# Broadcasting softmax reciprocals in four transfers, with another written-out instruction order

## The chip, the cores and the metric

The kernel runs on one core of a Trainium2 chip. A core has engines that work beside each other, each on an instruction queue of its own and in the order of that queue: TensorE (PE in the profile) multiplies matrices, VectorE (DVE) and ScalarE (ACT) work element by element and read TensorE's results from its accumulator memory, GpSimd (POOL) works element by element on the main on-chip memory, and SyncE (SP) does nothing here but issue DMA transfers. The transfers themselves run on 16 DMA engines that all queues share. Semaphores tie the queues together. The metric is the device time of one execution in microseconds (us); smaller is better.

## What is computed

A parallel block: attention and a gated feed-forward network read the same normalised input, and both results are added to the residual.

```python
x  = A_x                                  # 1 x 2048 x 512, bf16
xn = _layernorm(x)
# attention, 32 heads of 16
q, k, v = split_heads(xn @ A_wqkv)
p = softmax(q @ k^T * 16**-0.5)           # 32 x 2048 x 2048
attention = merge_heads(p @ v) @ A_wo
# gated network, 512 -> 1792 -> 512
gate = xn @ B_W_gate
h = relu(gate) * (xn @ B_W_up)
out = x + attention + h @ B_W_down
```

## The kernel before

**Tiles and stages.** The 2048 rows are normalised in 16 tiles of 128 and transposed once (`xnT`). Attention goes over four blocks of 512 queries, in each over four groups of eight heads, in each over the even and the odd heads (`ee`): 32 attention blocks of four heads, numbered 0 to 31, each over 16 tiles of 128 keys. For one key tile TensorE makes the scores of the four heads (`score()`). Mostly two heads' scores form a unit of 128 x 1024, whose exponential is one ScalarE instruction (L1418): 706 such units in all. For 159 key tiles (`QUAD_AT`) all four heads' exponentials are made elsewhere: VectorE turns the scores into the bits of an exponential by scale and shift (L1373, four to a key tile), and POOL (L1388) or VectorE (L1392) makes two shifted copies whose sum corrects it. TensorE then multiplies the exponentials by `v_aug`, the values with a column of ones beside them, so that the sum of the exponentials, the softmax's denominator, comes out beside the result. Between these, TensorE does the projections, the gated network and the output rows; all its chains of 128 rows are split into two halves of 64 rows, each half four matmuls of 64 x 32 weights against 512 columns. Such a group of four is called a half product below.

**Normalising a block** (`normalise()`). For each of the first 31 blocks, n = 0 to 30:

1. VectorE copies the accumulated block to `o_sb` (L1251).
2. SP issues a transfer of the four denominator rows into a 128 x 16 tile, `rsum<-o_sb` (L1267).
3. VectorE takes the reciprocals, `rrec<-rsum` (L1268).
4. SP issues a transfer of these to memory off the core, `rec_scr<-rrec` (L1269), 4 rows of 512.
5. SP issues the broadcast `rb<-rec_scr` (L1272): each of the four rows to 32 partitions, 256 KB.
6. POOL multiplies `o_sb` by `rb` (L1280 for even, L1285 for odd blocks; the latter's result is moved by four small transfers, L1289, tile `x_sb<-oT`).

The last block is normalised at the end of the kernel without transfers (`normalise_last()`).

**The order is data.** No engine's queue follows the loops. `PLAN` is a packed string of 8302 places: it says in which order the kernel's 8290 operations and 12 blank matmuls stand, and which buffer each tile gets. `Graph.run()` unpacks it, puts every operation at the end of its engine's queue, and adds the waits that the order and the buffers need. `Graph.emit()` gives semaphores and writes the instructions; a weight load is left out where the half of TensorE holds the weights already. SP has one queue for all 429 transfers, in the plan's order: it waits for what a transfer needs before it issues that transfer or any behind it. Each transfer adds 16 to the semaphore of its stream when it has landed; the broadcasts have the streams `n3`, 0 to 3 by turns.

Scores of units have two places of 128 x 1024 in the accumulator memory, by turns: TensorE writes a unit's scores when ScalarE is done with the unit two before. Everything else shares four places of 128 x 512.

Of the kernel before, what the change touches and what calls it, by code (L numbers as in the profile page):

```python
# [16 lines left out]
S = 2048  # L17
D = 512
H = 32
# [117 lines left out]
    "XK^8Qm=;@6?&E1w4;ASpBH0*GVS2hdWk}{&R_pdr@~(ke#k7!%u$(0<+!aou6u_E)Q2GT?sfe6>R|8P4Qua%7;Q@IQ!S+BB-KEGgL{QdbBek+HIcapk(Gf2zR`j-pmt@A0WXS}IT6tp&%C?9#{Yu5*7@`S4Sw}AG"
    "C{+R~^@-A!(>7YEE%J6pw{zu`E~;X;s}v!nw^3+ZMx)|++8=}5BuO&6a!MyaZ+$b@oo=vpOLm;7Lp(E{hMlx-tVfpEPL0g_i>T{Gxtrubp=e3YGmhew?guE4Wb&7kHcl%i7Ry+%f@nCo)vL_<6~`}1Wv<xfS0+Nn"
    "R4hWQcvR4!ycJWR3(~)YuPeU))(Un816m|0tr?B7vTtJ>J&x|W7?>D@<gExRHnfeFD;%ek6*gPafl}UYRnmm*RS+YuN>xwpe>jCHlqvESg^|C~iO7vk#UYo{#K`Rvs}}6oL@o-Iw$K&(n2Km9<v^EzEZOA7k8OXb"
    "Ko&>ZAdovqKFW|-4HZ$v@r~>?i6w{ZD#i)4TxePI49X@|DN_t=qV6z=O+}2(7|rUKu#y9{plc9iW7%e2VFxYzQ#lnl=$dC;H>OC|ouyRXA1UBe7O!+DD9PtXQl$eIsnTYG(*Z;d5h*id>q1^B{b}XakhNJAV4!pd"  # L140
    "l*4KE(XEzlW2&v-X6i`NaLFemtaUH4mIt#Pld@AlY&Rg21&cX7jA5iN>Gl~)i^!~F1&W>(Rz9bdD%v(t$3m5kTP3KRmeM~H{=ZYzirJ#1Lp`U|<BDELR8U(n9w}#M3Z67bK6wyjVAHuG$BrT@4n1VfMU>>|CWZ|m"
    "0H$pc$IkO4Wv5Msh)CY?ut2c=k8%d496RXpSY~Z3SxHy99hA?8*r|+sB%+XpgtSUt$)`q=ZU{NmlDCpbJ{=&tDrJW#Do0TA0<3%I<P%UCU7{pcX^9<VlH68yKy))8W0=lkfoD5^-Ju903s3|~GF|8pp<@<S!sT;P"
    "mSXa;j&kUxoR`YXrQBh=I*^pZQn^TrO4WF8CowNqR28|lKt-*Q<O<Izw5N3Yv<{0%p>IjoJdj>Ss&qb}><ke*p8-y%vYcJYSuV{~7G4o5LZBQ;Bjq$!ls5!KjFy()zdWT*xocEBqntS^-6CrxWR@fiFrwwDVl$}g"
    "`X!~ekrTHP+x@d+<aB0NupwTn*zAAmsZ^<CNbjmi6`SyX_OTV@AfKNpCku?2{t8lsc9PuLF?1;nr2I@k=>c`8`tq4M%S`q>MADsvb4tfu>2Z%1DnD4N<Q-1>XDdaukt&rDsiId=Dx1=@=`8%`WP<zuNK6MydAOuw"
    "KshubR6L?#bwoa&sMy9=JSL%sX`Jqaf>nOZL9FLh_U4j&+${$Yl-(vhr)537R$c@t>$6f%gosK>XMLbliTmWtQy$kSyF#F>TIr-nk`%v7lHBW5I>MKUh^yd$N(lSkC{^UMZkXa(rH@n&(JDPbtT+bI9hXZL4bMN2"
    "t~e``-KlhjI#{r>${v7-^dXE?u^HE$tH`RzX~}k;IwI5+Sw`QCAdsjKGu=ySm7_>4JC2~|V_Nojfu1Hva_7SiSVVUE^p9<FajQ7{t3YJMSzx8pCZ*e`+{$n|5dBk^MXpj|mvz=vad{{^%9R(S=g91#WTj0s?J_{u"
    "R<I3{SgC;1E+2F%Do_6uHN}4p%2=5YD<1ID6BtEr`B?#{+Z9!ASSqi`Rc<9Kw|q+5s*ppaE>0%c%Kf$6v1xdw0tZSD0u@{fmHPRASwSin<h@P>9moe$712<JSAH&8(Q-=4b6=_QA)_Sg&!C}&$~ht_%^SJEwTG+p"
    "%=4dA)45USuz&Vzm7u2d?o#Ckkvdf?r?eyiS2?{ot^yYvCssUCmkWX<=@6?>k0t#3=d~Kte@lP|B%#K@i##u0a}flCKfGvA4z-^Ndb}+ZK&{uHM~2%7T0JfPtG@3jJVjvl72i{7@Gpd4$pBOBS7e3ILq|c4?t&%$"
# [1326 lines left out]
```

## Time and profile before

| | |
|---|---|
| time, median of 3 executions | 680.99 us (680.63 to 682.62) |
| the profiled execution: its time | 681.0 us |
| its span, first to last instruction | 678.1 us |
| granted TensorE clock | 1.0 of full speed |
| SP's transfers | 429, of them 31 broadcasts of 256 KB |

The profile is of one execution. Its page gives each engine's busy time, the chain of work that ended last, and the costliest groups of instructions; other views of the same trace list who waited for whom, the instructions of an engine in order of time (the timeline), the transfers, and the busy times in chosen stretches. TensorE's matmuls are pipelined and their ends are modelled, so that a busy TensorE need not be at its peak.

### The profile page before, as it was taken

Reading aid. Unit: us, or ns where it says so; the run is one execution under the profiler, and the core shown is the slowest. Engines: PE = TensorE matmul, PEld = TensorE weight load, DVE = VectorE, ACT = ScalarE, POOL = GpSimd, SP = SyncE. Lnnn points to the kernel's source line nnn. Section 1 sums busy time; section 2 is a strip of 40 time slices with the busy share of each in tenths; the row PEclk is TensorE's granted clock in tenths of the full one; section 3 lists DMA queues with packets and bytes.
Section 4 is the critical chain, followed back from the end, with each engine's and each line's share of the span. In section 5 each row is a group of like instructions: output and inputs, shape, how many; then the busy total and the mean of one; then the engine's idle time right before and its main releaser. Section 6 shows DMA issues by size and latency. Waiting matters only on the chain.

```text
span 678.1 us, 46986 instructions
## 1 busy us (share of the span) xinstructions
PE 668.2 (99%) x22358; PEld 392.7 (58%) x21562; DVE 615.1 (91%) x1042; ACT 657.9 (97%) x718; POOL 511.7 (75%) x519
## 2 busy tenths in 40 slices
PE   8999999999999999989999999999999999999998
PEld 3555555566656666555555656555665565565554
DVE  9957899999999999889999989999999899999795
ACT  6999999999999999989999999999999999999995
POOL 3313657877788787888788878888888968888982
PEclk9999999999999999999999999999999999999999
DMA  7321221123121111111111112011112212101121
GB/s 218 66 50 29 60 68 44 47 66 93 47 85 35 48 28 54 39 47 47 51 49 34 52 30 59 17 40 40 58 28 73 61 33 72 39 23 38 33 64 58
DMA packets 55947, 35.97 MB, mean 53 GB/s; under 512 B 19336, under 2 KB 51784, under 8 KB 55752
## 3 DMA queue, kind: packets, MB, share of 16 engines
q1 hardware_dynamic: 55464, 32.71, 17.3%
q8 instruction: 171, 2.80, 1.7%
q10 hardware_dynamic: 288, 0.26, 0.1%
q14 instruction: 24, 0.20, 0.1%
HBM read 26.35 MB, written 2.35 MB: 42 GB/s over the span
## 4 chain that ended last, share of the span: by engine, by line
PE 91%; DVE 5%; DMA 2%; POOL 1%; issue 0%; SPq 0%; ACT 0%; DVEq 0%; POOLq 0%
PE ps L263 91%; DVE qd L1373 1%; DVE stats L758 1%; DVE xn_sb L771 1%; DMA rsum<-o_sb 1%; DMA xnT<-xn_sb 1%; POOL qd L1388 0%; DVE v_aug L909 0%; DMA rec_scr<-rrec 0%; DMA x_sb<-in_A_x_dram 0%; DVE qd L1392 0%; DVE qT L985 0%; DVE kT L902 0%; DVE mv L759 0%; DVE xnT L812 0%
## 5 line engine op out<-in xcount | busy, mean ns | idle before, releaser
L1418 ACT ACTIVATE ring<-ps 128x1024 bf16<-128x1024 f32 x706 | 651.4, 1079 | 6.2 <-PE ps L263 5.3
L1388 POOL TENSOR_TENSOR qd<-qd,ints 128x512 int32<-128x512 int32 x458 | 462.0, 1039 | 131.3 <-DVE qd L1392 81.0
L263 PE MATMUL ps<-qT,kT 64*32 64x512 bf16 x8192 | 466.6, 374 | 3.5 <-DVE qd L1373 2.4
L1373 DVE TENSOR_SCALAR qd<-ps 128x512 int16<-128x512 f32 x636 | 412.3, 684 | 36.2 <-PE ps L263 32.3
L263 PE MATMUL ps<-qd,v_aug 64*32 64x512 bf16 x3816 | 310.3, 375 | 0.1
L263 PE MATMUL ps<-ring,v_aug 64*32 64x512 bf16 x2824 | 244.2, 375 | 0.0
L1353 PEld LDWEIGHTS <-kT 64*32 64x32 bf16 x8032 | 170.9, 92 | 101.7 <-issue 15.5
L1325 PEld LDWEIGHTS <-v_aug 64*32 64x32 bf16 x6004 | 144.8, 92 | 71.8 <-issue 11.2
L263 PE MATMUL ps<-xnT,wgs 64*32 64x512 bf16 x1792 | 140.5, 374 | 0.2 <-DVE qd L1373 0.2
L263 PE MATMUL ps<-xnT,wus 64*32 64x512 bf16 x1792 | 137.3, 375 | 0.4 <-issue 0.2
L1392 DVE TENSOR_SCALAR qd<-qd 128x2048 int16<-128x2048 int16 x89 | 61.9, 701 | 1.2 <-PE ps L263 0.8
L842 PEld LDWEIGHTS <-wus 64*32 64x32 bf16 x1792 | 44.1, 91 | 23.7 <-issue 4.9
L842 PEld LDWEIGHTS <-wgs 64*32 64x32 bf16 x1792 | 43.2, 91 | 22.9 <-issue 3.8
L263 PE MATMUL ps<-Wd,hT 64*32 64x512 bf16 x608 | 55.3, 375 | 0.1
L842 PEld LDWEIGHTS <-hT 64*32 64x32 bf16 x1440 | 35.2, 92 | 21.1 <-issue 4.2
L263 PE MATMUL ps<-Wo_p,x_sb 64*32 64x512 bf16 x480 | 44.8, 375 | 0.0
L1057 DVE COPY up_sb<-ps 128x512 f32<-128x512 f32 x56 | 38.4, 686 | 3.4 <-PE ps L263 3.0
L263 PE MATMUL ps<-Wv,hT 64*32 64x512 bf16 x448 | 41.3, 375 | 0.0
L263 PE MATMUL ps<-Wv,xnT 64*32 64x512 bf16 x576 | 36.7, 374 | 0.5 <-DVE v_aug L909 0.3
L263 PE MATMUL ps<-xnT,Wq 64*32 64x512 bf16 x480 | 37.1, 375 | 0.0
L263 PE MATMUL ps<-xnT,Wk 64*32 64x512 bf16 x480 | 35.8, 374 | 0.3 <-DVE xnT L812 0.3
L263 PE MATMUL ps<-Wk,hT 64*32 64x512 bf16 x384 | 35.8, 375 | 0.0
(73 smaller groups left out, 306.5 us busy)
## 6 DMA issues: line engine op xcount, KB each, us to landing
rb<-rec_scr SPq DMA_DIRECT2D x31, 256.0 KB
wus<-in_B_W_up_dram SPq DMA_DIRECT2D x38, 128.0 KB, 2.9
wgs<-in_B_W_gate_dram SPq DMA_DIRECT2D x38, 128.0 KB, 2.7
xr_sb<-in_A_x_dram SPq DMA_DIRECT2D x16, 128.0 KB, 3.1
qT<-qf SPq DMA_DIRECT2D x120, 16.0 KB, 2.8
out_dram<-xn_sb SPq DMA_DIRECT2D x14, 128.0 KB, 3.2
x_sb<-in_A_x_dram SPq DMA_DIRECT2D x8, 128.0 KB, 2.8
x_sb<-oT SPq DMA_DIRECT2D x60, 16.0 KB, 3.0
```

The costliest lines, as they stand in the source:

```text
L263: return e.add_instruction(mybir.InstMatmult(name=e.bass.get_next_instruction_name(), engine=mybir.EngineType.PE, ins=[e.lower_ap(x), e.lo ...
L758: G.op("DVE", 580, lambda e, m=m: e.bn_stats(stats[:, m, :], xs(m)), reads=[t_xm[m]], writes=[t_st], prio=pr, order=last_xn if m == 4 else ())
L771: G.op("DVE", 320, lambda e, m=m, t=t_n: e.tensor_scalar(xn_sb[:, t.slot, :], xs(m), mv[:, m, 0:1], rstd[:, m:m + 1], op0=ALU.subtract, op ...
L842: e.ldweights(w()[rows, 32 * j:32 * j + 32], tile_position=(rows.start, 32 * j))
L1057: G.op("DVE", 603, lambda e: e.tensor_copy(up_sb[:, tup.slot, :], bank_of(tu)), reads=[tu], writes=[tup], prio=-590)
L1325: e.ldweights(vs(j), tile_position=(64 * half, 32 * j))
L1353: e.ldweights(ks(m), tile_position=(64 * half, 32 * m))
L1373: G.op("DVE", 601, lambda e, j=j, tx=tx: e.tensor_scalar(qd[:, tq.slot, 512 * j:512 * j + 512], ps[:, BANK[tx.slot], :], IBIAS[3], 0.0, op ...
L1388: G.op("POOL", POOL_NS / POOL_PIECES + 60, lambda e, x=x, n=n, c=slice(i * m, i * m + m): e.tensor_tensor(x().bitcast(I32)[:, c], raw().bi ...
L1392: G.op("DVE", 600, lambda e, n=n, x=x: e.tensor_scalar(x(), raw(), float(SHIFTS[n + 1]), None, op0=ALU.add), reads=[ti, tq], writes=[t], p ...
L1418: exp_ops[u] = G.op("ACT", 904, lambda e, tr=tr, k0=k0: e.activation(ring[:, tr.slot, :, :], ps[:, 4 * k0:4 * k0 + 2, :], ACTF.Exp, scale= ...
```

## The change

**The broadcast.** `PIECES = {"n3": 4}`. Where one transfer took a source of [4, 32 copies, 512] to 128 partitions, four transfers take one row each, [32 copies, 512], to 32 partitions. The four are issued one after the other at the broadcast's place in SP's queue; each adds 16 to the stream's semaphore, and who waits for a broadcast waits for 64 where it was 16. The bytes are the same. SP issues 522 transfers where it issued 429.

**The order.** `PLAN` is another one with the same 8290 operations and 12 blank matmuls; `PLAN_OPS` stays. ScalarE's queue is the same in every place. Of TensorE's 5597 places 4745 hold another operation at the same number, of VectorE's 1042 383, of POOL's 515 418, of SP's 429 382; nothing differs ahead of TensorE's place 71, VectorE's 63, POOL's 16 and SP's 22. Most buffers change as well. In the two orders stand:

| read from the two orders | before | after |
|---|---|---|
| half products from one unit's last scores to the next unit's, 705 intervals: mean | 7.81 | 7.81 |
| their standard deviation | 1.32 | 1.11 |
| intervals of 10 or more | 64 | 26 |
| `rsum` transfers at most 2 places behind a broadcast in SP's queue (of 31) | 10 | 2 |
| `rsum` transfers at most 4 places behind one | 16 | 5 |
| blocks with at most 2 units between the plan's places of `rsum` and of its reciprocal | 10 | 13 |
| units between these two for block 11 | 2 | 17 |
| groups of four weight loads on the two halves | 5357 | 5273 |
| TensorE operations behind the last scores | 62 | 61 |

```diff
 CARRIED = []
+PIECES = {"n3": 4}
...
                 if e == "SP":
-                    o.sem = (dsem[o.stream], 16 * (o.val + 1))
+                    o.sem = (dsem[o.stream], 16 * PIECES.get(o.stream[0], 1) * (o.val + 1))
...
-        fin = [(dsem[s], 16 * n) for s, n in streams.items()]
+        fin = [(dsem[s], 16 * PIECES.get(s[0], 1) * n) for s, n in streams.items()]
...
                 ins = o.fn(eng)
                 if e == "SP":
-                    ins.then_inc(o.sem[0], 16)
+                    for piece in ins if isinstance(ins, list) else [ins]:
+                        piece.then_inc(o.sem[0], 16)
...
-            dma(lambda e: e.dma_start(rb[:, trb.slot, :], rec_scr[n].unsqueeze(1).to_broadcast([4, 32, 512])), 520,
+            dma(lambda e: [e.dma_start(rb[32 * j:32 * j + 32, trb.slot, :], rec_scr[n, j:j + 1, :].to_broadcast([32, 512])) for j in range(PIECES["n3"])], 520,
                 reads=[tsc], writes=[trb], prio=pr - 50, stream=("n3", n % 4), name="n3")
```

The lines of the packed `PLAN` string, all but a few of which differ, are left out.

More of the change, by code (lines that the diff above doesn't have):

```diff
@@ L224 @@
[L224 to L226 removed]
+    "c-mcC2|!F;8@}(kGt)Fpi&QGv_dSuNLPGXPSraW}7fEHwPJ}Fd5`~n|A|X-8k}b-<@0GG;-;$Yo|8vg0cgp{vnmcECm*;)n=bY(dn1BD{$v<BDiF}b>kv|Pz;vX9_FNGh(3B2$g`71o;|5=b{s-HD@h5s?H#BHkQ"
@@ new lines @@
+    "OH=53;%?Qu>I@LRG<d}`4T|X;PJG0HWQS-mr!$=w=YnLYZcUyCX(wq9U^rm}(6xpCIELo{|DoeJG6d*;934V_=ER-oL{9eu-jtZela25{o)?3`>4K`WLo}8{{|1E2!n-qcJD#jZCz1yowHr8TM_w|Pz9a+bmOOCM"
+    "hWHsLx=UVBk3>Itx+KpD+Y*m}r+(qE(HF!DAcpYNEi#(UqF!+%jvOP!NX&;A5*kYV-@>NUO<sJH;b<K3roam?$euzRr5N*!?x_%S;KYCn`Jsl9VDn<e=`)TlPUlKF=4h}$T!H!lf|;C<Bq7Ok4dS5|1WUzbsE>jX"
+    "!XOeb2@!$^)Bz0=tQ1F(eMJkzh?1}L4Z$~tcq+avB3aD7XuA|D3F90iMutwrfT7RCN)<NNGGgSA7KwPLai$Z+y~qr$7*Ga8_l3|QI#gU=OfnuTI`~gQbmb-$U(KT9#6rWE77ZlmCMIzbWI(J_4u_itMVvukN47yi"
@@ new lines @@
+    "Qs@uWb%-doiFabgwLF8!7%j;I2O#<^*iV)t?*EmOy`^9XB!L7wc>E6j!_(p;Ka$`G!IKz8M44c;7Id6}?Z%ta$7D5%WFdTXDH>$0SSut~!p=0_40$4^jf6;-907O&P<bIvya+n{PlK@M0x(4EFf`?KJD%DuvH{rz"
+    "n<^xm(=A4$i?^hX;D5wzPK=tsDx#IVt_R>?&{fEHvIp4-KV=XH61iw8m(cmVNP_~vNYMYt$eUV$+=KvYbsQpA6U~PRB914~$HV9o9<M_q#fu(_-1$dAfP<YOE@%;n7k(4xk(Lf8)HOAqM`8d;HiYa776@xmx2PrL"
+    "J4aKA<4iXc!A)lgcoo+bs88Tc3_OBB0hvNX@fR(529<hZPKkx$It06wN*WKbNC=!+Y!Y6Hghw1nCXva%<%mW{h=O1$b&Yt&i<#yncxjP{UYbO$Fo!3sz)?EJjsq?@p^C9p40(x24bti)6-#&H88Ll$9+JvNs0x9L"
@@ new lines @@
+    "gguCxypDTum*NpMTq~rU_#t#cI-F*S8i0g1h2T)|Ndft-BpGMWFMa$~EAS^nK_J#7$rH^ojX3s<#D)?B{(*#$PywEU1T2w)6yhZ;LnEbSgzf_Z#%OVB#g;%FXMm}0>a_K7AQgv1hYXD?FD(fIjSIblCnX^)E=H3P"
+    "V=I`=)F4c$*rXOuyLL4?K-a>g+U7->Au<#7MXXsZlDep19|+Ln1U!o==5-20$TqDsPRk0$k>bO9YFM%u5{pQJmr&MXbC+Ntv@Ov-jf}7M3#wa0wa4@eh(kbV*E)qzQ*w%~))b{eAc<Ru6QvqY)rUa7^c_(<(KL|("
+    "7;%W^NB|D)HR3p$KxuQSElbYulE{=~F<&i189`z(I_&C%A8<M!=|fQt3QeD?AA$!loKQoN3c^leP|*~+v_zA%WPw(Yu7y%%3u57NLgN)XjMUY6QM?H8W(5AG4Fu8VE16515>PoKl$zvxb$hP?S8-jgW+L&E?`mF$"
@@ new lines @@
+    ")S8Ef>ZD7cu7(AbXVqF<)QytJmL!lU79_#TOY&UsUkEiNZz7gOQAt}X4?-K}Xk0+brdE^_f~b-Npcd6Y9Dc@eY<1d2z0T>7$cbSQ<0Yk9hjcO&R}nAjI#KS`=(3X17b6C`<}2`}B=Y%x6@K-LnpmrGN)ltFB_zm6"
+    "Jf}qxr<3SvkSIzC9F)HVj@BYU1Mz~O5W<EeTX~^~s0t986G)7}NF7>aIWfmnI{>9_+8G4G7c{%Tp|n-dg+wVzTQG=vOBzK7kUG|a4w#hJkto6m&(od);?}}JKx}f745O(M)+4wTx&Va??N^M*5d=U;;0R9a7__E9"
+    "1Siq}Cu#$+mjC~(%8PzV=MNGqjZD;ew4rJR+NLJcQzC7gqG}Ub1br+DDY4t}l28<m07BJJ&$YtYf)NN@5Z;7}Ks*Xi@CmC^lHkO-T9y-at)#cb(*Y+Qb3j*<x^o{RN>Wi*iLZsfG*ZAz=LDfy>JB>+1xhCZ(q%Z2"
@@ new lines @@
+    "1qH??$YXg)|B93+0GLBMIZTfiVk9_8xkyc!C(Cl87}pUC$JAs*DMpfW;`s-3R|Xv7#pWT-5|SwuDs7sA4CJNbkaTLH0fA~s0K9IZt`|x`rEVjku0>5*9bDagfe0iC0J^yXgNR2$8g0se0wh4df>x(FL?bCDNKh7f"
+    "BG&S{y46`J6r)5jH5pL%im4_>UT~Dx)h+D^yrfn+>B>bs;(~a7<a7sgv9*xKE(I0DKF&zl;Xoo=t*B51^{u7nR?%fr$6D#2EWE>rYOz|wiani^5T<iYlz^PB>j^<e5<0|wsLO!}y6T}~-zO0fj1>D5uhR@7JMg;x"
+    "B{pNJP3Tk}&okA`U%j=|e;MH*Cj><x9I3tVyr5ZylcA7ff&0Y$1%eSM2pCF;NIKJtlX;<$3L~nupX4|>HHzFU?he8+SEy8u|AzoU=Z&cN2~>5;Uy?)2|KIjWv1Fv`<OEnqmexRLO{H0_keQnDt){H37HoX=iC4Nj"
@@ new lines @@
+    "<g2xgR4Brsfu>KZOQj$Ig&x64_YLAj3s+s1x`UM{*?H+?K#!rkSazZ$)rwL?XbqCl0?qMAx)fuC#>a^VX)(z>=t3>r9EvY>s-T7zuhuAh^&KKtLyQVvr~+U(sFuKjqvDkn=p;~0VyM9!x&TX;VZ3f>Ar^@H_pX;H"
+    "Ql8aH@=omXoY-*jds2e~-8|B+>9K`Dy2=q$3&U!pI}D^tDLFYaf_Bg#sw(gyi4}=KD}qc^bmR<5*QUKf%L}O!4h~c=NO7*#(84CvX5rLI`zmelA~7)1sY85EATOk=GhVvxlp2e4#a(?PEL_AA-9rmWFo9l1iubXM"
+    "a47mK<Ev{2q*H`M%e-*iDdtnU2$s$wBBcljBh#u_;52fcVRZY|=t+pzagfwJB+XLYm<8j=(>InvKf)|h;|L^`zwRnnSG&TEC||>TX)$S8sfP<XO}x}$n7=aNDn^7dFp~1u0<Sxu2pUhg|J0ppsQwVSpxjDo$eiv{"
@@ new lines @@
+    "PRN_C(8Y@!QT&RhY5_OAt`%uTb`X1>bU&lJ36@Gm$7D4%2hZ31WJY%o`=@0v|5xC;4qT&cSAWE#+m2(z_)1XVbS;|J1BhPg_)QR(3@?dB9quSCg47u~;Tl~$U-7~fi-f7_lbsGp;*}%lV!-@!<gRfo05ueMwcj;j"
+    "@(<}(hfYU`|12j}CI>YR`_-Rs@gQASSGNXTDe=J9Xfm8oj)J(TQI5P&MZ!lF;-@;8B7{H)cdU}apxmStMRhg#3ZKD9w~zwc>3D_#(S9uh)qRwax~+8H7jHayRMQWs?@%QwTvACf)aq_<K)k}JsX=PImXx<}AgUpD"
+    "#XiT^Y_~N5SmWd>d`M88xl)^&pD;2t5)L(B!T)<07ut_lcf5GO(~1hGMzhm#hL$K!dOxo_i4de}rQ?No+To?6BZH(QG2#JCssY`3m@Y&Q%2dmWH-3UP5~3<m22S2<8;N*pR4vc{Q`FM^x$a>}J)ZgJnw}SL-gv3y"
@@ new lines @@
+    "la?kOZdhH`pyr*7^cfvJI7&LR#{G<_By<``C$@O0H&);3{ePKO5381ElFVlqMt8SfQ*>23RHKN+4^gY(T76Mi^OGl$L27PT<Ar$nB^}{~@zt7?Jknh()F^*JONkejyzXk27teGxo#Mq${c7%A{aLs$mxq6dTRJA`"
+    ">=QLp&ClJ%Yn6XAF{e9~F?@~k_(!-hLSA|1|8;WB;OMX*g-?1z5<dc*sy|y5kEFcxDX(-bCyF{9J90G{LiepU{QF;t0u+CL0t<*oZGh!imMgH8$@KrQoPHHFdM49j>%c2$SOR)vxP?rsr^SC2_Z!QeBCz~~pUE}&"
+    "3&P*Y03+=uWQNeg#xe!E3$^k4wcsm2eFVne5g6cYSpH_GYh9rL?+FU9L_HG$8uq-{6P>`T;P3bkR08xtv0Z9?H2-RlkJ@pHTWtZlJ^^i0<Iiet<;V%iP`|e3m*Q6`SgW42`TTBST%DgKu-mh}>Wlgl$jq8=Y}9<&"
@@ new lines @@
+    "`Y*q=va17?r}}Wm-wlIWu7Rjay>cVjUr_xvMAMbs42MG1pDg!Nr`8y<aM&disk>VN{P=$PgWE}qimOMV2(m2g^S=$r_Oap7!{3<-6Ex#l3)na;>+irnwN`|vjxK<iliL?+)W6!Q3lA8r04QkkME_5BI8mo=Ny5;2"
+    "RmzIqa2-_@I)!IiLj0aVnX+S9HUr^FBSpKF=;8!L3+OPdUc$2(TNHy}6KrVM-~RFK2WSl3=yaq?qZkDZB2;(LRZm|?OhSHW_wfU}&qJ@Nnl;v({9Tc}4s4lu`QDOXbs(IH7*;vAHn(E&)m`!H!aw(SU4}pt^-W!w"
+    "T?lEb#-iZ0i<Tmzan`UzA05=(TOwZq#rqS-A4G2;D6Gy5=QnS5z(j=FHFZFtNx#2XM_uXoxdf%~$V;R2-_zf;MH6^gZ@e}=zp`0aL}PflsDJN}u}QCP!I?R->*H$ee6scOO_;iPV4wL7V0vOhyOrNZX&&f%@9{6_"
@@ new lines @@
+    "l?M+e8hyP9J@W=_gcnh&%Cq)`(0j|w>6(}=U066iq^QNz7yf(mp{VnDRnX>}Nx3ROSu3(@$EqGg+QrO$1XGH+Q%61x7zk%lhu=K<GGH~FTJ$W{Gk%20cNR`Ymp)URoL$JHR=Wl?U*QHCdC)LlmF(9|`?q`iZ0^{W"
+    "nxorcQ9()I#U?#He=e#Wz}>^cga2%s%R2vA4_9Y!iqlt5MmcI`c|+Hp7dFkgUDUZ_jw#3>@Zyr;wwEnGDvY23+Wuend#Nd71}3+$)8vj$UAElj;*u=eJq<sA?fW-i4m}mV8lT<{g)2tDO}jGJQ(wp2gY(Lh2aP|V"
+    "ya`FaU0&ByTkYthugP@F?|IO-(x(1fO(}GVd>b0!*`gF|lU%KW##q9E9WLim!S3Da|9-+X!%?p$9(dTOsMY4Vpss4}@7znC-}9qVdErcd>*p$ujI*1MqM@%*p+nTfrv^<Lm)YEJadwJ=dwQ-nG^*g9G_@*$8)n_#"
@@ L229 @@
+    "tvt-~n7#}}NlGdoh!Q1s8BzI31*@77$Fj6l*<hT|O)*R9D+C!yGAzf5CKO$dCCY*76zsQP41o%*Ttg*oHkij%B5=u)BrGfyO?q--i%^(=i&{ouq(p=}fyy?7p$Uexrl}?--pRqtk}PAaVk8Zuz#%gtObMid@QT<d"
+    "eJW^#vSAntYdlh}riz9ooMS9VGenq)szw>jJ&Tlt0|}}y0uhx!m}?CPQm~X!2sMP*{{e<{%2x")
 class Pool:
```

171 lines of the change are left out of this document (69 added, 102 removed).

## The prediction

> **What bounds the kernel.** I read the page's busy times first, then the same by stretches of 100 us away from the two ends.
>
> ```profile
> span 678.1 us, 46986 instructions
> ...
> PE 668.2 (99%) x22358; PEld 392.7 (58%) x21562; DVE 615.1 (91%) x1042; ACT 657.9 (97%) x718; POOL 511.7 (75%) x519
> ```
>
> ```profile
> core 0: us, PE busy (x) PEld busy (x) DVE busy (x) ACT busy (x) POOL busy (x), PEclk, DMA share, GB/s
> 50.00:100.00 50.00, 49.94 (x1676) 27.30 (x1652) 42.77 (x68) 50.00 (x55) 26.30 (x28) 1.00 0.19 53
> 100.00:200.00 100.00, 99.72 (x3361) 60.06 (x3249) 95.25 (x159) 99.60 (x109) 78.55 (x78) 1.00 0.22 61
> 200.00:300.00 100.00, 97.81 (x3376) 59.22 (x3176) 91.02 (x151) 97.35 (x106) 82.54 (x82) 1.00 0.16 46
> 300.00:400.00 100.00, 99.84 (x3384) 58.19 (x3252) 96.91 (x162) 98.78 (x108) 80.46 (x80) 1.00 0.15 43
> 400.00:500.00 100.00, 99.82 (x3432) 60.12 (x3296) 91.63 (x151) 99.87 (x110) 86.22 (x85) 1.00 0.15 43
> 500.00:600.00 100.00, 99.56 (x3388) 59.57 (x3244) 93.60 (x154) 99.30 (x109) 84.00 (x84) 1.00 0.18 51
> 600.00:650.00 50.00, 49.49 (x1720) 29.31 (x1660) 43.54 (x71) 49.61 (x55) 43.88 (x44) 1.00 0.14 40
> ```
>
> Two engines are full, TensorE and ScalarE, and they hang together: ScalarE may not run ahead of the scores, TensorE may not write scores more than two units ahead. ScalarE's share says how well the order works, because its queue is nothing but units. The best stretch (400 to 500) starts 110 of them, one each 100/110 = 0.909 us. At that pace 600 us would hold 660 units; the seven rows hold 55 + 109 + 106 + 108 + 110 + 109 + 55 = 652. So a better order can win about 8 x 0.909 = 7.3 us between 50 and 650 us, if its pace were the best one throughout. That is the prize; the change leaves ScalarE's work and queue alone, so nothing else shortens that stretch.
>
> The waits say what breaks the pace.
>
> ```profile
> ACT ring L1418 <- PE ps L263: 5.3, 11, 2.0
> ...
> PE ps L263 <- DVE qd L1373: 2.6, 3, 2.0
> DVE rrec L1268 <- DMA rsum<-o_sb: 2.5, 2, 2.1
> ...
> POOL x_sb L1280 <- DMA rb<-rec_scr: 1.1, 1, 1.1
> ```
>
> The columns are the total, the number of times and the longest. Three waits of 2.0 to 2.1 us are one event: VectorE stands before a reciprocal whose denominators have not landed, so TensorE gets no free place, so ScalarE gets no scores. The timelines of VectorE and SP and the chain that ended last show it.
>
> ```profile
> 288.28 0.68 DVE L1373 TENSOR_SCALAR qd<-ps 128x512 int16<-128x512 f32 x1
> 291.10 0.25 DVE L1268 RECIPROCAL rrec<-rsum 128x16 f32<-128x16 f32 x1 [2.14 <-DMA rsum<-o_sb]
> ```
>
> ```profile
> 285.21 0.58 SPq L1272 DMA_DIRECT2D rb<-rec_scr  x1
> 285.84 0.47 SPq L1118 DMA_DIRECT2D out_dram<-xn_sb  x1
> 286.35 0.59 SPq L1267 DMA_DIRECT2D rsum<-o_sb  x1
> ```
>
> ```profile
> 286.35 4.72 DMA rsum<-o_sb
> ```
>
> The `rsum` transfer, 8 KB, took 4.72 us; it was issued 1.14 us behind a broadcast. The other 8 KB transfer of the chain, `rec_scr<-rrec`, took 2.4 us at the median and 3.6 at most:
>
> ```profile
> DMA to landing us min/median/max: 1.4/2.4/3.6
> ```
>
> **The broadcast in four.** A stretch in which a broadcast moves almost alone shows how it runs today.
>
> ```profile
> 78.10:80.90 2.80, 2.80 (x98) 1.76 (x89) 2.02 (x4) 2.80 (x5) 1.90 (x2) 1.00 0.25 94
> ```
>
> In 2.80 us 94 GB/s moved, 263 KB: the 256 KB of the broadcast and little else. The DMA share is 0.25, so a quarter of the 16 engines worked, four of them, full the whole time. A small transfer that needs one of these four stands behind up to 2.8 us of packets; that is the 4.72 less the usual 2 or so. [...] By my own terms I only need that a broadcast cannot hold four engines longer than it does now.
>
> When does the whole broadcast land? The pieces follow each other by the pitch of issue, 285.84 - 285.21 = 0.63 us, so the last goes out 3 x 0.63 = 1.9 us after the first. Its own landing is bounded by the nearest transfers:
>
> ```profile
> rb<-rec_scr SPq DMA_DIRECT2D x31, 256.0 KB
> wus<-in_B_W_up_dram SPq DMA_DIRECT2D x38, 128.0 KB, 2.9
> ...
> qT<-qf SPq DMA_DIRECT2D x120, 16.0 KB, 2.8
> ```
>
> Between 2.8 and 2.9 us, so 1.9 + 2.9 = 4.8 us from the first issue. Today the packets alone end 80.90 - 76.75 = 4.15 us after the issue of this broadcast at 76.75 (its row stands here), and the landing is later still.
>
> ```profile
> 76.75 0.60 SPq L1272 DMA_DIRECT2D rb<-rec_scr  x1
> ```
>
> The multiply gets its reciprocals when it got them before, to within half a microsecond. POOL waited for a broadcast once, 1.1 us (row above); I cost this at nothing, with 1.1 us either way as bounds. [...]
>
> **What SP pays.** 31 x 3 = 93 more issues at 0.63 us are 59 us on SP's queue. They lie beside SP's waits:
>
> ```profile
> SPq L1269 <- DVE rrec L1268: 53.6, 15, 10.6
> SPq L1289 <- POOL oT L1285: 44.9, 10, 8.3
> SPq L892 <- DVE qf L886: 41.2, 10, 12.5
> SPq L1267 <- DVE qd L1373: 38.2, 14, 8.6
> ...
> SPq L1272 <- DMA rec_scr<-rrec: 26.7, 17, 3.2
> ```
>
> The first four alone are 178 us. On average it is hidden. Without cover, each broadcast puts what is queued behind it (query pieces L892, weights L1044, the next `rsum`) 1.9 us later; I take nothing and keep, as the far end, one stall the size of the one seen, 2.1 us. Where SP is early it costs nothing and gains nothing.
>
> **The order.** Term one: the stall at 289 us goes. Block 11's reciprocal has 17 units between it and its `rsum` in the new order, where it had 2; 17 x 0.909 = 15 us cover a transfer of 2 to 5. And 2 `rsum` transfers stand within two places behind a broadcast, where 10 did. I take off the whole 2.1 us. What is late next? At that place nothing in the rows: VectorE's idle time there has no second releaser. The least it can give is 0, if another reciprocal stalls in its stead.
>
> Term two: scores come more evenly. Intervals of ten or more half products between two units' scores fall from 64 to 26, by 59%. In the table 7.3 - 2.1 = 5.2 us are lost beside the stall. If all of it hung on such intervals, 0.59 x 5.2 = 3.1 us come back; if none, 0. I take 1.2, nearer to nothing, because TensorE's own waits are ended by VectorE's evictions and not by a long interval, and VectorE is 91% busy with an unchanged amount of work. Below nothing is possible too: a changed order has its own unlucky places; one event of 2.1 us is the largest seen in 678.
>
> Term three: the ends. The first 71 places of TensorE are the same, and behind the last scores stand 61 operations for 62. I take nothing.
>
> The sum is made against the profiled execution: 681.0 - 2.1 - 1.2 = 677.7 us. Its time equals the median of 680.99, and its span of 678.1 leaves 2.9 us around it that nothing here touches.
>
> **Rivals.**
>
> *A full gain.* Both terms at their best and the pace of 400 to 500 us throughout: 681.0 - 7.3 = 673.7. For it: every measure of evenness in the order improved. Against: VectorE, whose waiting ends score places, keeps its 615 us.
>
> *Hidden, and late elsewhere.* The transfers were hidden anyway (the one wait of 1.1 us), and the stall goes but a weight load comes late, since weights stand behind broadcasts that now take 1.9 us longer to issue. Idle time ahead of weight loads of L842 exists, the longest 2.4 us, though the profile names no releaser for it ("issue"), so that 2.4 is the nearest row and not a proven wait for a transfer:
>
> ```profile
> PEld L842 <- issue: 20.5, 76, 2.4
> ```
>
> One of these gives 677.7 + 2.4 = 680.1, no change that can be measured; also the case in which the new order is simply no better.
>
> *The reciprocal again, slower.* VectorE's queue stalls at every reciprocal whose denominators are late, at up to 2.1 us each. In the new order 13 blocks have at most 2 units (1.8 us) between `rsum` and reciprocal, for 10 before; a broadcast ahead of SP's `rsum` now delays its issue by 1.9 us, which is just that. From 3.3/2.1 = 1.6, so from two such events, the gain is gone; four make 677.7 + 8.4 = 686.1, three 684.0. Against it: ten blocks that tight made two waits in all, of 2.5 us together, and only two `rsum` now follow a broadcast closely.
>
> [...]
>
> **Chances.** The forecast, 675.5 to 678.9, 0.44; the full gain, below 675.5, 0.12; hidden or late elsewhere, 679.0 to 683.0, 0.27; the reciprocal again 0.13; pieces that do not overlap 0.04. About 0.3% (2.0 us) is what a measurement of this kernel can tell from no change. Faster by more: 0.44 + 0.12 = 0.56; within: 0.27; slower by more: 0.17. The range goes from the full gain, 673.7, to 683.0, the upper edge of no change: it leaves out most of the 0.17 and the last of the full gain.
>
> **What would show it.** Right: no wait of VectorE for `rsum` above 0.5 us; 109 or 110 units in the stretch from 200 to 300 us; a DMA share well above 0.25 while a broadcast moves; more than 652 units from 50 to 650 us; 336 fewer weight loads (84 groups of four). Wrong: new idle time before L1268, POOL waiting for `rb` many times, TensorE's weight loads waiting longer for L1044's transfers, or fewer units at equal VectorE time.

## The result, and the profile after

| | before | after |
|---|---|---|
| time, median of 4 executions | 681.81 us (680.63 to 682.88) | 676.35 us (675.45 to 676.5) |
| ratio of the two, 95% interval | | 0.9918 [0.9893, 0.9943] |
| the profiled execution: its time, its span | 681.0, 678.1 us | 675.45, 673.5 us |

The changed kernel is faster by 0.8%, 5.6 us of 681.8. Its lines are numbered two higher than before (L1274 is the broadcast, L1269 `rsum`, L1270 the reciprocal, L1420 the units).

The page of the changed kernel, its busy times, answers to the first lines of the prediction:

```profile
span 673.5 us, 46743 instructions
...
PE 666.5 (99%) x22358; PEld 381.7 (57%) x21226; DVE 616.3 (92%) x1042; ACT 656.0 (97%) x718; POOL 512.5 (76%) x519
```

The work is the same to within 2 us on every engine but one: weight loads (PEld) went from 21562 to 21226, 336 fewer. So the 4.6 us of span are idle time and slow places that are gone, not work. Busy times by stretch, the whole middle in one piece, first the kernel before and then the changed one (the columns are as in the prediction: length, busy time and count of PE, PEld, DVE, ACT and POOL, then the clock, the DMA share and GB/s):

```profile
50.00:650.00 600.00, 596.18 (x20264) 353.76 (x19516) 554.72 (x909) 594.51 (x645) 481.94 (x475) 1.00 0.17 48
```

```profile
50.00:650.00 600.00, 599.87 (x20480) 347.36 (x19412) 560.70 (x917) 598.56 (x652) 486.11 (x478) 1.00 0.18 48
...
200.00:300.00 100.00, 99.94 (x3464) 57.81 (x3184) 93.58 (x154) 99.87 (x109) 85.98 (x85) 1.00 0.17 48
```

ScalarE started 652 units in these 600 us where it started 645, at 0.909 us each 6.4 us. (In one piece a unit that spans an edge of 100 us counts once, so these two numbers are lower than sums over the pieces; by the pieces of the prediction's table it is 661 for 652.) The stretch from 200 to 300 us, 106 before, holds 109. A part of the 6.4 us is given back ahead of it; the stretch from 30 to 50 us, before and after:

```profile
30.00:50.00 20.00, 19.90 (x680) 11.56 (x652) 13.19 (x21) 19.92 (x23) 5.59 (x8) 1.00 0.30 54
```

```profile
30.00:50.00 20.00, 18.35 (x634) 9.93 (x608) 13.31 (x20) 18.61 (x21) 5.29 (x6) 1.00 0.26 62
```

TensorE and ScalarE work 1.3 to 1.6 us less here, and two units fewer start. The waits of the changed kernel name it: VectorE's key copy `kT`, and what ScalarE still waits for in all.

```profile
ACT ring L1420 <- PE ps L264: 2.5, 5, 1.2
...
PE ps L264 <- DVE kT L904: 1.4, 1, 1.4
```

No row for `rsum` or `rb` is left. The issues and landings, after (count, size and median us from issue to landing), with all broadcasts together in the last line:

```profile
rb<-rec_scr SPq DMA_DIRECT2D x124, 64.0 KB, 2.2
...
qT<-qf SPq DMA_DIRECT2D x120, 16.0 KB, 1.9
```

```profile
DMA to landing us min/median/max: 1.9/2.2/3.5
```

A piece lands in 2.2 us though four go out together. The query pieces `qT`, which have nothing to do with the broadcast, land in 1.9 us where they took 2.8. Those issued within 4 us of a broadcast's issue (of its last piece's, in the changed kernel) took 4.1 us at the median before (22 of the 120), the others 2.6; in the changed kernel it is 2.5 (41) and 1.9. Part of that differs from chip to chip: on those of the experiments they took 2.9 us in the new order with one transfer (e2 below) and 2.4 with four (e8).

### The profile page after: what moved, and what is told of

The parts are those of the page before. It is cut to its first block, busy times and chain, and to the rows that moved or that the text cites. A ratio compares the mean times of both kernels' runs of the same rounds, so it can differ in the third digit from the quotient of the medians.

```text
span 673.5 us, 46743 instructions
## 1 busy us (share of the span) xinstructions
PE 666.5 (99%) x22358; PEld 381.7 (57%) x21226; DVE 616.3 (92%) x1042; ACT 656.0 (97%) x718; POOL 512.5 (76%) x519
## 4 chain that ended last, share of the span: by engine, by line
PE 94%; DVE 4%; DMA 1%; POOL 0%; issue 0%; ACT 0%; SPq 0%
PE ps L264 94%; DVE stats L760 1%; DVE xn_sb L773 1%; DMA xnT<-xn_sb 1%; DMA x_sb<-in_A_x_dram 0%; DVE v_aug L911 0%; DVE qT L987 0%; DVE qd L1375 0%; DVE xnT L814 0%; DVE kT L904 0%; DVE mv L761 0%; POOL rstd L755 0%; ACT xn_sb L1219 0%; DVE kT L1001 0%; SPq L689 0%
## 5 line engine op out<-in xcount | busy, mean ns | idle before, releaser
L1420 ACT ACTIVATE ring<-ps 128x1024 bf16<-128x1024 f32 x706 | 649.7, 1129 | 2.9 <-PE ps L264 2.5
L264 PE MATMUL ps<-qT,kT 64*32 64x512 bf16 x8192 | 458.7, 374 | 0.2
L264 PE MATMUL ps<-qd,v_aug 64*32 64x512 bf16 x3816 | 302.0, 375 | 0.0
L264 PE MATMUL ps<-ring,v_aug 64*32 64x512 bf16 x2824 | 242.3, 375 | 1.4 <-DVE kT L904 1.4
L1355 PEld LDWEIGHTS <-kT 64*32 64x32 bf16 x7944 | 163.8, 92 | 105.1 <-issue 14.9
L1327 PEld LDWEIGHTS <-v_aug 64*32 64x32 bf16 x5756 | 138.5, 91 | 73.4 <-issue 11.4
L264 PE MATMUL ps<-xnT,wgs 64*32 64x512 bf16 x1792 | 140.5, 374 | 0.0
L264 PE MATMUL ps<-xnT,wus 64*32 64x512 bf16 x1792 | 137.2, 374 | 0.0
L264 PE MATMUL ps<-Wd,hT 64*32 64x512 bf16 x608 | 54.5, 375 | 0.0
L264 PE MATMUL ps<-Wo_p,x_sb 64*32 64x512 bf16 x480 | 42.8, 375 | 0.0
L264 PE MATMUL ps<-Wv,hT 64*32 64x512 bf16 x448 | 40.9, 375 | 0.0
L264 PE MATMUL ps<-xnT,Wq 64*32 64x512 bf16 x480 | 36.6, 375 | 0.2
L264 PE MATMUL ps<-Wv,xnT 64*32 64x512 bf16 x576 | 36.3, 374 | 0.1
L264 PE MATMUL ps<-Wk,hT 64*32 64x512 bf16 x384 | 35.5, 375 | 0.0
L264 PE MATMUL ps<-xnT,Wk 64*32 64x512 bf16 x480 | 34.0, 374 | 0.4 <-DMA xnT<-xn_sb 0.2
```

The source lines that it names most:

```text
L264: return e.add_instruction(mybir.InstMatmult(name=e.bass.get_next_instruction_name(), engine=mybir.EngineType.PE, ins=[e.lower_ap(x), e.lo ...
L1327: e.ldweights(vs(j), tile_position=(64 * half, 32 * j))
L1355: e.ldweights(ks(m), tile_position=(64 * half, 32 * m))
L1420: exp_ops[u] = G.op("ACT", 904, lambda e, tr=tr, k0=k0: e.activation(ring[:, tr.slot, :, :], ps[:, 4 * k0:4 * k0 + 2, :], ACTF.Exp, scale= ...
```

## The experiments

The twelve kernels ran on other chips than the pair above, where the kernel before took about 687 us; so only ratios to it are compared, and a microsecond below is a ratio times 687. "Old order" is the order before, "new order" the changed kernel's. Moves within an order were made behind the plan, with the buffers that the plan gives: operation x goes right behind operation y.

```diff
+for x, y in MOVES:
+    seq.remove(x)
+    seq.insert(seq.index(y) + 1, x)
```

| kernel | order, pieces | further edit | ratio to before, 95% interval |
|---|---|---|---|
| e1_split_alone | old, 4 | | 0.9965 [0.9933, 0.9998] |
| e2_order_alone | new, 1 | | 0.9936 [0.9914, 0.9958] |
| e3_late_reciprocal | old, 1 | block 11's reciprocal later | 0.9971 [0.9945, 0.9997] |
| e9_split_and_late | old, 4 | the same | 0.9948 [0.9919, 0.9977] |
| e8_after_again | new, 4 | the changed kernel itself | 0.9903 [0.9873, 0.9932] |
| e4_two_pieces | new, 2 | | 1.0110 [1.0079, 1.0141] |
| e11_eight_pieces | new, 8 | | 1.0021 [0.9993, 1.0049] |
| e6_long_intervals | new, 4 | 41 units' scores later | 0.9961 [0.9938, 0.9985] |
| e7_short_intervals | old, 1 | 38 units' scores sooner | 1.0035 [1.0007, 1.0064] |
| e10_split_late_short | old, 4 | e9's edit and e7's | 0.9964 [0.9937, 0.9991] |
| e5_key_copy_first | new, 4 | key copy sooner | 0.9886 [0.9861, 0.9912] |
| e12_three_scores | new, 4 | e5's edit, three scores sooner | 0.9878 [0.9844, 0.9912] |

### The two halves of the change alone

e1_split_alone: the new kernel's code with the plan of before.

```diff
+PIECES = {"n3": 4}
```

> The old order with the broadcast in four pieces. If the order brings the gain and the split only shortens the stall at 289 us (the denominators of block 11 no longer stand behind four full DMA engines, but leave 1.2 us later), VectorE's wait there falls from 2.1 to about 0.5 us and the time by 1 to 2 us: ratio to before 0.997 to 0.9985. If the split itself brings most of it, because all small transfers land sooner, the ratio is near 0.993. If SP's 93 more issues hurt an order that was not made for them, it is above 1.000.

It gained 2.4 us, with an interval from 0.1 to 4.6. By the last step of their semaphores in the traces, no `rsum` transfer took over 2.1 us any more, where 7 of the 31 took over 3 us before. Still the same reciprocal waits, 1.30 us and not the 0.5 that were expected. SP's and VectorE's timelines of e1_split_alone:

```profile
285.22 2.46 SPq L1274 DMA_DIRECT2D rb<-rec_scr  x4
...
288.19 0.60 SPq L1269 DMA_DIRECT2D rsum<-o_sb  x1
```

```profile
290.09 0.25 DVE L1270 RECIPROCAL rrec<-rsum 128x16 f32<-128x16 f32 x1 [1.30 <-DMA rsum<-o_sb]
```

In the old order `rsum` stands behind the broadcast; it now lands in 1.9 us instead of 4.7, and leaves 288.19 - 286.35 = 1.84 us later. Of the stall of 2.14 us, 1.30 are left. The later issue is SP's price, and it shows a second time: `PE ps L264 <- DMA qT<-qf: 1.0, 1, 1.0`, a wait for a query piece that the kernel before does not have.

e2_order_alone: the changed kernel with its broadcast in one transfer.

```diff
-PIECES = {"n3": 4}
+PIECES = {"n3": 1}
...
+            dma(lambda e: [e.dma_start(rb[:, trb.slot, :], rec_scr[n].unsqueeze(1).to_broadcast([4, 32, 512]))], 520,
```

> The new order with the broadcast as one transfer of four rows. If the order brings the gain: ratio 0.993 to 0.995, no reciprocal waiting over 1 us, transfers of 16 KB for the queries landing in 2.8 us at the median as before. If the split is what counts: ratio 0.997 or more, and waits for rsum of 2 us and over are back.

It gained 4.4 us; no reciprocal waits, and the `qT` pieces land in 2.9 us, about as before. The two halves add up: 2.4 + 4.4 = 6.8, and the whole, e8_after_again, gives 6.7; each of the three is known to some 2 us either way.

> The changed kernel once more, unchanged, as the measure for the other three kernels on the same chip: ratio to before 0.989 to 0.994, no reciprocal waiting over 0.5 us, TensorE waiting 1.4 us for the key copy at 35 us.

### The stall by itself

e3_late_reciprocal moves block 11's reciprocal behind the next five instructions of VectorE in the old order.

```diff
+MOVES = ((3450, 3635),)
```

> The old order with one change: the reciprocal of block 11 stands five VectorE instructions later. Term one of the prediction: the 2.1 us stall goes and nothing comes in its place, ratio 0.997 (2.1 us of 681), 108 or more units between 200 and 300 us for 106. Rival: a stall elsewhere takes its place, ratio 0.999 to 1.000.

It gained 2.0 us, with an interval from 0.2 to 3.8. The stretch from 200 to 300 us holds 107 units, one more than before and one less than expected; TensorE works 2.02 us more in it and ScalarE 1.62. Another reciprocal (L1277 in this kernel) has begun to wait, as the rival had it:

```profile
200.00:300.00 100.00, 99.83 (x3404) 59.31 (x3208) 92.52 (x153) 98.97 (x107) 83.67 (x83) 1.00 0.16 45
```

```profile
DVE rrec L1277 <- DMA rsum<-o_sb: 1.6, 1, 1.6
```

e9_split_and_late adds the four pieces, so that the reciprocal is late and all `rsum` transfers are quick.

```diff
+PIECES = {"n3": 4}
+MOVES = ((3450, 3635),)
```

> The old order with the broadcast in four pieces and the reciprocal of block 11 five VectorE instructions later: both repairs of the stall at 289 us and of late transfers, without the new order. If these are most of what the change does: ratio 0.990 to 0.993. If the rest of the new order, its evenness among it, is worth 3 us or more, as the changed kernel with long intervals suggests: 0.994 to 0.997.

No reciprocal waits, and it gained 3.6 us. So what repairs the transfers is worth about 3.6 of the 6.7 us, and 3.1 come from the rest of the order. The two intervals, [0.9919, 0.9977] and [0.9873, 0.9932], overlap a little: the split is rough.

### Two pieces and eight

e4_two_pieces takes two rows to 64 partitions in each of two transfers.

```diff
-PIECES = {"n3": 4}
+PIECES = {"n3": 2}
...
+e.dma_start(rb[64 * j:64 * j + 64, trb.slot, :], rec_scr[n, 2 * j:2 * j + 2, :].unsqueeze(1).to_broadcast([2, 32, 512]))
```

> The changed kernel with the broadcast as two transfers of two rows each. If the outermost dimension (two rows) sets the number of DMA engines, two engines carry everything: about 5.7 us of packets for a broadcast, a DMA share of 0.13 where it moves alone, landings of rsum behind it over 6 us, multiplies waiting for rb, ratio 0.995 to 1.005. If the 64 partitions set it, all 16 engines work: the broadcast lands within 4 us as in four pieces, SP has 62 issues fewer, and the ratio is the changed kernel's.

It is slower than before by 1.1%, and 12 us slower than the same order with one transfer. A stretch, SP's and VectorE's timelines and the waits of e4_two_pieces say why.

```profile
94.00:97.00 3.00, 3.00 (x116) 1.98 (x104) 2.97 (x5) 3.00 (x4) 1.79 (x3) 1.00 0.16 44
```

```profile
95.14 0.60 SPq L1269 DMA_DIRECT2D rsum<-o_sb  x1
```

```profile
101.82 0.25 DVE L1270 RECIPROCAL rrec<-rsum 128x16 f32<-128x16 f32 x1 [2.75 <-DMA rsum<-o_sb]
```

```profile
POOL x_sb L1282 <- DMA rb<-rec_scr: 9.8, 5, 4.1
POOL oT L1287 <- DMA rb<-rec_scr: 4.1, 3, 2.3
DVE rrec L1270 <- DMA rsum<-o_sb: 2.8, 1, 2.8
```

132 KB moved in 3 us, half the rate of before's 263 KB in 2.80 us, with a DMA share of 0.16 where before had 0.25 (0.125 would be two engines of 16; the small transfers are in the 0.16). The ratio is above the whole range that was expected for that case. The `rsum` behind them landed 101.82 - 95.14 = 6.7 us after its issue. The traces show the difference in two more ways. Of the 2 KB packets of a broadcast mostly four move at once in the kernel before (at 78 us), two here (at 94 us), though two transfers are out, and up to 17 in the changed kernel (at 407 us; the records of two packets can overlap a little). And a transfer raises its semaphore in 5 steps before, in 3 here and in 16 as a piece; an `rsum` transfer has 5 steps before and after. So by these runs it isn't the number of transfers that helps: with two, of two packets at once, the kernel is 1.1% slower than before, with four, of 16 steps each, 1.0% faster (e8). The outermost dimension of the source is 4, 2 and 32 in the three; that this dimension sets the number of engines, as the first case of the expectation has it, agrees with the three but was not shown, as no run changes it alone.

e11_eight_pieces takes half the copies of a row in each of eight transfers, 32 KB to 16 partitions.

```diff
-PIECES = {"n3": 4}
+PIECES = {"n3": 8}
...
+e.dma_start(rb[16 * j:16 * j + 16, trb.slot, :], rec_scr[n, j // 2:j // 2 + 1, :].to_broadcast([16, 512]))
```

> The changed kernel with the broadcast in eight pieces of half a row to 16 partitions, 124 issues more on SP. Each broadcast then holds SP for some 4.5 us instead of 2.3. If SP's issues are hidden in its waits: the changed kernel's ratio, 0.990. If what stands behind a broadcast comes late (the price that the prediction put at one stall of 2.1 us for four pieces): 0.993 to 1.000, with waits of VectorE for rsum or of TensorE for query transfers.

It loses 8.1 us against four pieces, more than expected. Each piece still lands in 2.1 us, but SP takes 4.8 us at the median to issue eight, and the whole broadcast lands 7.0 us after its first issue. The waits of e11_eight_pieces are those for the broadcast itself and for things that stand behind it in SP's queue:

```profile
POOL x_sb L1282 <- DMA rb<-rec_scr: 6.1, 4, 2.3
...
DVE rrec L1270 <- DMA rsum<-o_sb: 1.9, 2, 1.6
PE ps L264 <- DMA qT<-qf: 1.6, 1, 1.6
```

So SP's cover of waits, 178 us on its first four rows, bears 93 more issues and not 217, in this order.

### How even the scores come

e6_long_intervals takes the changed kernel and puts the scores of 41 units behind the next two half products, so that 64 intervals of ten or more stand in the order again (standard deviation 1.29, before 1.32).

```diff
+MOVES = ((3555, 2934), (3556, 3555), (2543, 2427), (2544, 2543),
...
```

> The changed kernel with 41 units' scores put behind the two half products that followed them, so that 64 intervals have ten half products or more, as in the old order, for 26. If evenness of the scores is part of the order's gain (term two of the prediction, 1.2 us, or the 2.1 us that such intervals lost less in the changed kernel's trace): 0.002 to 0.005 above the changed kernel's ratio. If evenness is worth nothing, as the old order with shortened intervals suggests: equal to it within 0.001, and the gain of the order lies in its distances to transfers.

Against e8_after_again it loses 0.0058, 4.0 us (some 2.6 either way), with intervals that do not touch, and no reciprocal waits in it. ScalarE's waits for scores, e6_long_intervals and then e8_after_again:

```profile
ACT ring L1429 <- PE ps L265: 6.7, 21, 1.2
```

```profile
ACT ring L1420 <- PE ps L264: 3.9, 8, 1.2
```

(L1429 and L265 are there what L1420 and L264 are here.) 13 more waits, 2.8 us of the 4.0: a score held back by two half products costs 0.1 us on average.

e7_short_intervals does the reverse in the old order: 38 units' scores are pulled ahead, and the intervals of ten or more fall from 64 to 26, as the change has them.

```diff
+MOVES = ((2133, 1724), (2134, 2133), (7660, 7496), (7661, 7660),
...
```

> The old order with units' scores pulled ahead of one to three half products where the interval before them was ten or more: 26 such intervals for 64, as in the new order; the stall at 289 us stays. Term two of the prediction alone: 1.2 us, at most 3.1, ratio 0.9955 to 0.998. Rival: evenness of scores is worth nothing, ratio 0.9993 to 1.001.

It is 2.4 us slower than before, which neither side of the expectation had. Its waits have two reciprocals late, `DVE rrec L1277 <- DMA rsum<-o_sb: 4.5, 2, 2.7`; behind the longer one, 2.70 us, the granted clock was 0.50 for 3.41 us (last section). To take the stall away, e10_split_late_short makes the same moves in e9's kernel, where no reciprocal waits.

```diff
 PIECES = {"n3": 4}
-MOVES = ((3450, 3635),)
+MOVES = ((2133, 1724), (2134, 2133), (7660, 7496), (7661, 7660),
...
+    (3008, 2390), (3009, 3008), (3450, 3635))
```

> The kernel of the run before with units' scores pulled ahead as in the old order with shortened intervals (26 intervals of ten or more half products for 64). If evenness is worth something where no reciprocal stalls: 0.002 to 0.005 below the run before. If it is worth something only in an order made for it, because whatever is put behind the scores comes late in its stead: equal to it or above.

Nothing was gained: 0.9964 beside e9's 0.9948, and one reciprocal waits again, 1.2 us. Holding scores back costs; pulling them ahead, past the work that other engines wait for, brings nothing by itself. The number of long intervals is then not what the rest of the order won by, though it goes with it.

### The head

e5_key_copy_first moves VectorE's key copy ahead of two normalisations in the changed kernel.

```diff
+MOVES = ((166, 158), (179, 166), (177, 179))
```

> The changed kernel with VectorE's copy of the keys (kT) at 35 us ahead of two normalisations of xn instead of behind them. TensorE's wait of 1.4 us there should fall to 0.3 us or less and ScalarE's loss of 1.3 us with it: 1 us, 0.0015 below the changed kernel's ratio. Rival: the normalisations and their transposes come 0.7 us later and give the time back: equal to it.

VectorE's and TensorE's timelines of the changed kernel show what it undoes, and then the stretches, after and e5:

```profile
31.90 3.10 DVE L773 TENSOR_SCALAR xn_sb<-hT,mv,rstd 128x512 bf16<-128x512 bf16 x4
34.92 0.68 DVE L904 CAST kT<-ps 128x512 bf16<-128x512 f32 x1
```

```profile
35.65 0.38 PE L264 MATMUL ps<-ring,v_aug 64*32 64x512 bf16 x4 [1.38 <-DVE kT L904]
```

```profile
30.00:40.00 10.00, 8.48 (x302) 5.04 (x281) 7.54 (x12) 8.78 (x10) 5.29 (x6) 1.00 0.27 56
```

```profile
30.00:40.00 10.00, 9.45 (x328) 5.43 (x316) 7.70 (x14) 9.46 (x11) 5.25 (x6) 1.00 0.40 57
```

In the new order the copy stands behind four normalisations, 3.10 us, and TensorE waits 1.38 us for it. In e5 the wait is gone, and the two full engines work 0.97 and 0.68 us more of these ten. The ratio is lower by 0.0017, 1.2 us, about that size but not to be told apart from e8's by their intervals.

e12_three_scores adds three units' scores (395, 401, 405, each with a loss of 0.5 to 0.6 us in the changed kernel) pulled ahead.

```diff
-MOVES = ((166, 158), (179, 166), (177, 179))
+MOVES = ((166, 158), (179, 166), (177, 179), (4758, 4163), (4759, 4758),
...
```

> The kernel with the key copy first, and the scores of three units (395, 401, 405 counted from 0) pulled ahead of three to five half products: the intervals of 14 before them become 9, 11 and 9. In the changed kernel ScalarE loses 0.56, 0.50 and 0.62 us there, 1.7 in all. If the length of an interval is what costs: 1 to 1.5 us less than with the key copy alone, ratio near 0.987. If what is put behind comes late in its stead, as in the old order: 0.9886 or above.

It can't be told apart from e5. One of the three losses falls from 0.56 to 0.08 us, one from 0.50 to 0.33, one stays whole; but over the 14 units around them ScalarE's loss is 1.9 us, where e5 has 1.8. Nothing was gained at this place. These two have the lowest ratios of all, and only their distance to the kernel before is certain.

## Why the prediction was right, and where not

**Direction and size.** Right: 677.7 forecast, 676.35 measured, inside the bounds of the forecast's own case (675.5 to 678.9). Against the profiled execution 3.3 us were foretold and 5.5 came; 4.6 of them lie in the span, and the rest around it (2.9 us before, 1.95 after), where the change does nothing: in other runs of the kernel before that part took 1.75 to 3.0 us. That 0.9 us is chance, and the two errors of the terms below have opposite signs: that 677.7 lies so close to 676.35 is in part luck.

**What bounds.** Right. Two engines at full load, and the start of units as the measure: 7 more of them in the middle, and neither engine's own work less by more than 1.9 us.

**Term one, the stall: 2.1 us.** Right in place and size. From the start of unit 300 to that of unit 310, counted from 0, the changed kernel, e2 and e3 each take 2.1 us less than the kernel before, and e1 takes 0.8 us less. As a whole time, e3 measured 2.0, but only to 1.8 us either way and with another reciprocal late. Its cause had two parts, as the rows said: the slow landing behind the broadcast, 4.72 us, and the place right after it. The split alone (e1) repaired the first and made the second worse by 1.84 us; the order alone (e2) took both away for this block. Block 11's `rsum` now leaves 24.8 us ahead of its reciprocal. SP's and VectorE's timelines of the changed kernel:

```profile
279.11 0.60 SPq L1269 DMA_DIRECT2D rsum<-o_sb  x1
```

```profile
303.93 0.24 DVE L1270 RECIPROCAL rrec<-rsum 128x16 f32<-128x16 f32 x1
```

**Term two, evenness: 1.2 us, mis-sized.** This is where most of the rest of the difference between the pair's traces lies. From the start times of the 706 units in both traces, those more than 0.17 us over the pitch of 0.904 us lost 10.9 us before and 5.7 after: 5.2 us won, of which the stall is 2.1 and 3.1 are not, with what the head lost already taken off. That e8 and e9 also lie 3.1 us apart does not make it sure: their ratios leave 0.3 to 6 us, and e8, the same kernel as the changed one on another chip, loses 8.6 us by the same measure of its trace. The prediction's upper end was 3.1, and it chose 1.2 because TensorE's waits ended with VectorE's evictions. That reason was the step that failed: e6 shows that late scores cost 4.0 us on their own with VectorE's work unchanged. But the upper end was not right for its reason either, since e7 and e10 had the intervals and not the gain. Which places of the order, outside the transfers and the scores' intervals, bring the 3.1 us is not settled.

**Term three, the ends at nothing: wrong by 1.4 us.** The first 71 places of TensorE and 63 of VectorE are the same, so the step looked no further; the loss stands just behind, at 35 us, in the order of VectorE. It was within the sum's own uncertainty and of the other sign than term two's error.

**The broadcast at nothing.** The landing was forecast at 4.8 us from the first issue, as late as before. By the last step of the semaphore in the traces, the whole broadcast lands 4.2 us after its first issue (median of 31), where the one transfer took 4.9: in four pieces it comes a little sooner. POOL's one wait for it is gone. Left out of the sum was what else lands behind a broadcast: the sooner landing of `qT`, 1.9 us for 2.8, came unforeseen. It has no price of its own here, as no wait for `qT` was on before's list.

**SP at nothing.** Right for four pieces in the new order: no wait for `qT`, weights or `rsum` is on its list. It holds for that order alone. e1 shows the price in one not made for it (1.84 us at the stall, 1.0 us for a query piece), e11 that eight pieces are too many.

**The rivals.** *Hidden, and late elsewhere* did not come. *The reciprocal again* did not either, though 13 blocks are tight: the tightest, which the changed kernel's timelines of SP and VectorE show here, has 99.14 - 96.66 = 2.48 us, and its transfer landed in 1.9.

```profile
93.83 2.23 SPq L1274 DMA_DIRECT2D rb<-rec_scr  x4
...
96.66 0.60 SPq L1269 DMA_DIRECT2D rsum<-o_sb  x1
```

```profile
99.14 0.24 DVE L1270 RECIPROCAL rrec<-rsum 128x16 f32<-128x16 f32 x1
```

It is 0.6 us behind a broadcast, and not late. Its mechanism is real all the same: e1, e3, e4, e7, e10 and e11 all have a reciprocal that waits 1.2 to 2.8 us. *Pieces that do not overlap*, 0.04 of the chances, was the author's estimate, and no run shows it: a piece lands in 2.2 us at the median and 3.5 at most, while its fellows move, and the whole broadcast in 4.2. One transfer of 256 KB (e2, 0.9936) lost to four of 64 KB (e8, 0.9903) by the ratios, though their intervals overlap. Eight of 32 KB did lose (e11, 1.0021), but by the time of the issues, 4.8 us: each of them lands as soon, in 2.1 us.

**The marks.** Right: no wait for `rsum`, 109 units from 200 to 300 us, more units in the middle, 336 fewer weight loads. One mark was badly chosen, and no row of before spoke for it: a DMA share well above 0.25 while a broadcast moves. A stretch of the changed kernel with little else in it:

```profile
407.30:409.50 2.20, 2.20 (x84) 1.22 (x72) 1.72 (x3) 2.16 (x4) 0.77 (x2) 1.00 0.37 97
```

With 2.23 / 4 = 0.56 us between two pieces (the row at 93.83), 65.5 KB each, no more than 117 GB/s can come; the single transfer had 94. The gain is not in rate. In this stretch the number of 2 KB packets that move at once goes up and down between one and 17, where the single transfer had four or five for 2.55 of its 2.80 us. A better mark would have been the landing of the next small transfer.

## What to carry to other kernels

Read the number of engines that a broadcast uses from the DMA share while it moves alone (0.25 here, four of 16), and look at what stands behind it: here the damage was done to the next small transfer, which landed in 4.72 us where 1.9 is the median, not to the broadcast. Here splitting it into four paid, and into eight it no longer did, with 4.8 us of issues that pushed later transfers past their moment; and an order written for one transfer has to be looked at again; here the two were worth 2.4 and 4.4 us, each to some 2 us either way, and by these ratios neither made the other needless. In these orders, where two engines are full, scores held back cost 4.0 us (e6), but scores pulled ahead, past work that other engines wait for, gained nothing (e10, e12).

## What the runs showed of the hardware

Behind some idle times of TensorE, of 2.1 to 2.9 us, its granted clock was 0.50 for 3.41 us, and so they cost more than their own length. In e7_short_intervals VectorE waits 2.70 us before the reciprocal at 295.83, and TensorE stands idle for 2.54. TensorE's timeline and the stretches behind it:

```profile
296.69 0.38 PE L264 MATMUL ps<-qT,kT 64*32 64x512 bf16 x4 [2.54 <-DVE qd L1382]
```

```profile
296.68:297.54 0.86, 0.85 (x28) 0.43 (x28) 0.86 (x2) 0.00 (x0) 0.34 (x1) 1.00 0.11 10
297.54:300.95 3.41, 3.41 (x72) 1.59 (x60) 2.34 (x4) 2.17 (x3) 3.41 (x4) 0.50 0.16 46
300.95:303.00 2.05, 2.05 (x88) 1.74 (x76) 1.61 (x3) 1.98 (x3) 0.52 (x1) 1.00 0.17 60
```

The column behind POOL is the clock: 0.50 of full speed for 3.41 us, with TensorE busy throughout. It started 72 matmuls in these 3.41 us, 21 a us, and 88 in the 2.05 us behind them, 43 a us: half of the 3.41, 1.7 us of its work, is lost there. The kernel before, behind its stall of 2.14 us, in which TensorE was idle for 1.98, kept its clock in the profiled execution:

```profile
291.00:293.00 2.00, 1.05 (x36) 0.53 (x32) 1.90 (x4) 0.15 (x1) 0.64 (x2) 1.00 0.07 8
293.00:295.00 2.00, 2.00 (x84) 1.43 (x76) 1.92 (x5) 2.00 (x3) 2.00 (x3) 1.00 0.11 29
```

In e4_two_pieces and e11_eight_pieces the same 3.41 us at 0.50 follow idle times of 2.85, 2.23 (e4) and 2.11 us (e11), and nothing follows one of 2.06 (e4). Whether the length of the idle time alone decides was not shown.

1.7 us of 680 lower the mean clock of a run to 0.9975. With the experiments, 41 of the 90 runs of the kernel before that count for the ratios show 0.998 or less, against 1 of 90 runs of the nine kernels whose stalls are shorter or gone (e1, e2, e3, e5, e6, e8, e9, e10, e12). On the four chips the medians of these runs of the kernel before were 0.9, 1.5, 2.0 and 2.4 us longer than those of its others. If the stall at 289 us lowered the clock in those 41, its removal is worth somewhat more than term one; where in those runs the clock fell, no trace shows.
